# All clamps of the first FFN's weights on GpSimd as (min, max), and the casts of the first block's g and of the first two blocks' x on ScalarE

## The chip, the core and the metric

The kernel runs on one core of one Trainium2 chip. The metric is the device time of one execution in microseconds, lower is better. The engines are TensorE (PE; PEld is its weight load), VectorE (DVE), ScalarE (ACT), GpSimd (POOL) and SyncE (SP), which issues the DMAs. Each engine has one queue of instructions, taken in order; engines wait for each other by semaphores.

## The reference

Attention with a causal window of 64 tokens (4 sequences of 576 tokens, 8 heads of 64), a first feed-forward layer with ELU, an RMS norm, and a second, gated feed-forward layer. The part that the change touches is the first layer:

```python
def _moe_ref(x, w_in, w_out):          # x [2304, 512], w_in [512, 2048], w_out [2048, 512]
    h = x @ w_in
    g = np.where(h > 0.0, h, np.exp(np.minimum(h, 0.0)) - 1.0)
    return g @ w_out
```

The inputs and the result are wider than what one matmul takes: the weights arrive in 8-byte words of which the kernel reads both 32-bit halves, and the matmuls run on pairs (a rounded part and the remainder).

## The kernel before, in words

Every matmul operand of the feed-forward layers is split in two: a rounded part (a cast to the matmul's type) and what is left (a subtraction). A product is then three matmuls: rounded by rounded, remainder by rounded, rounded by remainder.

*The feeder of weights* (class `Feeder`, object `fw1` for the first layer, with `pool=True`; `fwp` for the second, with `pool=False`). A unit is a 128 x 512 piece of `w_in` or `w_out`; the first layer has 32 of them. Each passes through three stages, one `step()` apart:

- `s1`: ACT makes the magnitude from the high half (L311, into a tile `wm`, of which there are three) and scales the low half in place (L312); then a clamp to `MAX_M` (L314), by DVE for even units and by POOL for odd ones where `pool` is set, always by DVE for the second layer; then DVE shifts and joins the halves (L316).
- `s2`: DVE sets the sign (L323), and `nc.any` casts the rounded part (L331), on ACT or DVE, whichever the planner picks.
- `s3`: the remainder is subtracted, by POOL in the first layer (L337).

A unit's raw tile is loaded by SP up to four units ahead (L304) and comes free after `s2`.

*The first layer* runs over 6 blocks of 384 tokens. In each block 16 steps f: `mm_in` (12 matmuls, L381) gives h in PSUM; `elu` makes g with two ACT steps (L399, L400) and one of DVE (L401), and `split_g` casts it (L390, through its argument `copy`, here always DVE) and subtracts (L391, DVE); two steps later (`LAG`) `mm_y` multiplies g by `w_out` (12 matmuls, L408). Only in block 0 are the units of `fw1` made: two `step()`s in each f. The split weights then stay for the other blocks. Beside each of the first five blocks runs the attention for the next one, in slots between the steps (`att_*`, L164 to L239), which fills the next x; `x_split` casts the 4 parts of x (L364, DVE) and subtracts (L365, DVE), for block 0 ahead of the loop and for each later block at the end of the block before.

*Blocks 1 to 4* also hold the preparation of the second layer's weights (`prep_matrix`, `prep_out`: `fwp.s1`, the sign, and combinations by POOL, written to DRAM). Then the second layer follows.

*Order.* The program's order is not the order on the engines: a planner lays the instructions out on the queues by a modelled timeline and also picks the engine of each `nc.any` operation. Once laid out, each queue is fixed.

Of the kernel before, what the change touches and what calls it, by code (L numbers as in the profile page):

```python
# [13 lines left out]
ALU = mybir.AluOpType  # L14
# [6 lines left out]
def kernel(  # L21
# [17 lines left out]
    nc = tc.nc  # L39
# [10 lines left out]
    BLOCKS1 = [384]*6  # L50
    MAX_M = (2.0 - 2.0 ** -20) * 2.0 ** 15 / 2.0 ** 112
# [26 lines left out]
    def psum(tag, bufs):  # L78
        if starting[0] and tag == "w":
            tag, bufs = (("w", 4), ("y", 4))[starting[1] % 2]  # L80
            starting[1] += 1
        return ps.tile([128, 512], F32, tag=tag, name=tag, bufs=bufs)
# [162 lines left out]
    def att_schedule(u0, n, xt, nslots, gap):  # L245

        tail = 4 + 2 * gap
        slots = {}

        def put(s, key, f):  # L250
            slots.setdefault(s, []).append((key, f))

        first = 2
        pitch = max(1.0, (nslots - 1 - tail - first) / max(1, n - 1))
        for i in range(n):
            u = u0 + i
            sb = first + int(i * pitch)
            put(sb - 2, 0, lambda u=u: att_a(u))
            put(sb, 1, lambda u=u: att_b(u))
            for h in range(2):  # L260
                e = sb + h * gap
                put(e, 0.5, lambda u=u, h=h: att_e(u, h))
                put(e + gap - 1, 3, lambda u=u, h=h: att_n(u, h))
                put(e + gap, 4, lambda u=u, h=h: att_c(u, h))
            put(sb + 2 * gap + 2, 5, lambda u=u, o=i * 128: att_d(u, xt, o))
        return {s: [f for _, f in sorted(v, key=lambda z: -z[0])] for s, v in slots.items()}
# [17 lines left out]
    class Feeder:  # L284
# [23 lines left out]
        def s1(self, i):  # L308
            lo, hi = self.r[i][:, :, 0], self.r[i][:, :, 1]
            m = mp.tile([128, 512], F32, tag="wm", name="wm", bufs=3)  # L310
            nc.scalar.activation(out=m, in_=hi.bitcast(F32), func=AF.Abs, scale=2.0 ** -112)  # L311
            nc.scalar.activation(out=lo, in_=lo.bitcast(U32), func=AF.Copy, scale=0.875 * 2.0 ** -29,  # L312
                bias=0.4999)
            (nc.gpsimd if self.pool and i % 2 else nc.vector).tensor_scalar(  # L314
                out=m, in0=m, scalar1=MAX_M, scalar2=None, op0=ALU.min)
            nc.vector.scalar_tensor_tensor(  # L316
                out=m.bitcast(I32), in0=m.bitcast(I32), scalar=3, in1=lo,
                op0=ALU.logical_shift_left, op1=ALU.bitwise_or)
            self.m[i] = m
# [37 lines left out]
                self.step()  # L357


    def x_split(xt, n):  # L360
        r = []
        for kk in range(KD):
            xk = mp.tile([128, 2, NMAX], F32R, tag=f"x{kk}", name=f"x{kk}")
            nc.vector.tensor_copy(out=xk[:, 0, :n], in_=xt[:, kk, :n])  # L364
            nc.vector.tensor_tensor(  # L365
                out=xk[:, 1, :n], in0=xt[:, kk, :n], in1=xk[:, 0, :n].bitcast(F32),
                op=ALU.subtract)
            r.append(xk)
        return r

    def mm_in(pt, wt, xs, n, by_k=False):

        seq = []
        for kk in range(KD):
            seq += [(kk, 0, 0), (kk, 1, 0)]
        for kk in range(KD):
            seq += [(kk, 0, 1)]
        if by_k:
            seq.sort(key=lambda z: z[0])
        for i, (kk, a, c) in enumerate(seq):  # L380
            nc.tensor.matmul(  # L381
                pt[:, :n], lhsT=wt[:, a, kk * 128:(kk + 1) * 128], rhs=xs[kk][:, c, :n],
                start=(i == 0), stop=(i == len(seq) - 1))

    def x_tile():
        return mp.tile([128, KD, NMAX], F32, tag="xt", name="xt")

    def split_g(src, n, copy):
        g = mp.tile([128, 2, NMAX], F32R, tag="g", name="g", bufs=1 + LAG)
        copy(out=g[:, 0, :n], in_=src[:, :n])  # L390
        nc.vector.tensor_tensor(  # L391
            out=g[:, 1, :n], in0=src[:, :n], in1=g[:, 0, :n].bitcast(F32), op=ALU.subtract)
        return g


    def elu(ph, n):

        e = mp.tile([128, NMAX], F32, tag="e", name="e", bufs=2)
        nc.scalar.activation(out=e[:, :n], in_=ph[:, :n], func=AF.Relu, scale=-1.0)  # L399
        nc.scalar.activation(out=e[:, :n], in_=e[:, :n], func=AF.Exp, scale=-1.0)  # L400
        nc.vector.scalar_tensor_tensor(  # L401
            out=e[:, :n], in0=e[:, :n], scalar=-1.0, in1=ph[:, :n], op0=ALU.add, op1=ALU.max)
        return split_g(e, n, nc.vector.tensor_copy)

    def mm_y(py, wt, g, n, first, last):
        for i, (a, c) in enumerate(((0, 0), (1, 0), (0, 1))):
            for m in range(KD):
                nc.tensor.matmul(  # L408
                    py[m][:, :n], lhsT=wt[:, a, m * 128:(m + 1) * 128], rhs=g[:, c, :n],
                    start=(first and i == 0), stop=(last and i == 2))  # L410
# [65 lines left out]
    def x_load(sb):  # L476
        t0 = 2 * NB * sb
        xa = mp.tile([128, 2, 2 * NB], F32, tag="xt", name="xa")
        xb = f2p.tile([128, 2, 2 * NB], F32, tag="xb", name="xb")
        for h, t in enumerate((xa, xb)):  # L480
            nc.sync.dma_start(out=t, in_=xspill[:, 2 * h:2 * h + 2, t0:t0 + 2 * NB])
        xab[0], xab[1] = xa, xb
# [126 lines left out]
    def p_load(n):  # L609
        i, j = n // 7, ORDER[n % 7]  # L610
        u = wp.tile([128, 2, 2, 256], F32R, tag="wu", name="pu")
        nc.sync.dma_start(
            out=u.rearrange("p a b c -> p (a b c)").bitcast(F32), in_=pspill[:, n, :])
        U[i, j] = u
# [139 lines left out]
    xt = x_tile()  # L754
# [7 lines left out]
        load_v(t)  # L762
    for s in range(NSTART):
        fw1.step()
    xs = x_split(xt, BLOCKS1[0])

    tok0 = 0
    pend = []
    nblk = len(BLOCKS1)
    for b, n in enumerate(BLOCKS1):  # L770
        last = b == nblk - 1
        slots = {}
        if not last:
            nn = BLOCKS1[b + 1]
            xt = x_tile()
            slots = att_schedule((tok0 + n) // 128, nn // 128, xt, 2 * F1 - 1, 3)
        else:
            att_stack.close()
            f2p = ctx.enter_context(tc.tile_pool(name="f2p", bufs=1))
            x_load(0)  # L780
            for j in range(AHEAD2):
                slots.setdefault(14 + 2 * j, []).append(lambda n=j: p_load(n))
            for j in range(len(prep_o) // 2):
                slots.setdefault(PS0 + (31 - PS0) * j // (2 * F2), []).append(prep_o.pop(0))
            xi = x_items()
            for j, fn in enumerate(xi[:5]):
                slots.setdefault(15 + 3 * j, []).append(fn)
            x_late += xi[5:]
        if b and not last:
            for i in range(PREP_PER):  # L790
                if prep:
                    slots.setdefault(PS0 + (31 - PS0) * i // PREP_PER, []).append(prep.pop(0))
        for i, f in enumerate(pend):
            slots.setdefault(NS0 + NSP * i, []).insert(0, f)
        py = [psum("y", 4) for _ in range(KD)]
        gs = {}

        def run_slot(s):
            for f in slots.get(s, []):
                f()  # L800

        for f in range(F1):
            fw1.until(("in", f))
            ph = psum("w", 4)
            mm_in(ph, wu[("in", f)], xs, n, f == F1 - 1)
            gs[f] = elu(ph, n)
            run_slot(2 * f)
            if f == F1 - 1 and not last:
                xs_next = x_split(xt, nn)
            if b == 0:  # L810
                fw1.step()
            if f >= LAG:
                fw1.until(("out", f - LAG))
                mm_y(py, wu[("out", f - LAG)], gs.pop(f - LAG), n, f == LAG, False)
            run_slot(2 * f + 1)
            if b == 0:
                fw1.step()
        for f in range(F1 - LAG, F1):
            fw1.until(("out", f))
            mm_y(py, wu[("out", f)], gs.pop(f), n, False, f == F1 - 1)  # L820
        if last:
            for fn in x_late:
                fn()
        pend = norm_items(py, n, tok0, last)
        if not last:
            xs = xs_next
        tok0 += n
# [87 lines left out]
```

## Time and profile before

| | |
|---|---|
| median of 3 runs | 968.45 us (966.33 to 969.38) |
| the profiled execution, its time | 967.15 us |
| its span, first to last instruction | 965.4 us |
| PE busy | 918.5 us (95%) |
| DVE busy | 650.4 us (67%) |
| ACT busy | 491.9 us (51%) |
| POOL busy | 211.8 us (22%) |

The profile is of one execution. An engine's busy time is the time in which it has an instruction at work; a wait is idle time of an engine put down to what ended last before it went on. Shares over the whole span mix stages: block 0 of the first layer, which alone makes weights, lies at about 40 to 143 us, the other blocks of the first layer up to about 540, the second layer from there to the end. A duration of DVE or POOL also holds time in which the instruction had begun and stood still.

### The profile page before, as it was taken

Reading aid. Unit: us, or ns where it says so; the run is one execution under the profiler, and the core shown is the slowest. Engines: PE = TensorE matmul, PEld = TensorE weight load, DVE = VectorE, ACT = ScalarE, POOL = GpSimd, SP = SyncE. Lnnn points to the kernel's source line nnn. Section 1 sums busy time; section 2 is a strip of 40 time slices with the busy share of each in tenths; the row PEclk is TensorE's granted clock in tenths of the full one; section 3 lists DMA queues with packets and bytes.
Section 4 is the critical chain, followed back from the end, with each engine's and each line's share of the span. In section 5 each row is a group of like instructions: output and inputs, shape, how many; then the busy total and the mean of one; then the engine's idle time right before and its main releaser. Section 6 shows DMA issues by size and latency. Waiting matters only on the chain.

```text
span 965.4 us, 16449 instructions
## 1 busy us (share of the span) xinstructions
PE 918.5 (95%) x5916; PEld 863.7 (89%) x5916; DVE 650.4 (67%) x1451; ACT 491.9 (51%) x1199; POOL 211.8 (22%) x228
## 2 busy tenths in 40 slices
PE   6678889999999999999999999999999999999998
PEld 5577789988889998899999999899998998998996
DVE  3899997858867786787788488178363276561461
ACT  5887755665666656566545456344141442341440
POOL 2465760146236114404402100200000000000000
PEclk9789989999999999999999999999999999999999
DMA  9556531765474265536438719781984737945621
GB/s 234 165 167 199 133 108 23 221 194 159 146 228 145 78 197 172 156 103 199 159 122 286 262 48 385 283 349 48 404 328 143 278 124 243 371 141 208 240 70 66
DMA packets 150402, 183.02 MB, mean 190 GB/s; under 512 B 81712, under 2 KB 111408, under 8 KB 150320
## 3 DMA queue, kind: packets, MB, share of 16 engines
q1 hardware_dynamic: 150320, 181.96, 57.3%
q8 instruction: 47, 0.77, 0.3%
q14 instruction: 35, 0.29, 0.1%
HBM read 144.18 MB, written 37.75 MB: 188 GB/s over the span
## 4 chain that ended last, share of the span: by engine, by line
PE 67%; DMA 6%; POOL 4%; ACT 4%; DVE 4%; issue 1%; SPq 0%; POOLq 0%; DVEq 0%; ACTq 0%
PE y L669 16%; PE w L669 12%; PE y L408 11%; PE w L381 10%; PE y L703 10%; PE w L703 5%; DMA pspill<-stg 5%; POOL stg L540 2%; ACT s L206 1%; ACT stg L539 1%; PE w L164 1%; POOL sw L569 1%; PE w L235 1%; PE w L222 1%; PE w L187 1%
## 5 line engine op out<-in xcount | busy, mean ns | idle before, releaser
L381 PE MATMUL w<-x,wu 128*128 128x384 f32 x1152 | 226.8, 345 | 15.3 <-DVE e L401 5.7
L408 PE MATMUL y<-g,wu 128*128 128x384 f32 x1152 | 223.7, 340 | 5.6 <-DVE g L390 3.0
L381 PEld LDWEIGHTS w<-x,wu 128*128 128x128 f32 x1152 | 203.8, 192 | 21.4 <-DVE e L401 6.1
L408 PEld LDWEIGHTS y<-g,wu 128*128 128x128 f32 x1152 | 198.6, 188 | 10.1 <-DVE g L390 4.2
L669 PE MATMUL y<-xw,pu 128*128 128x384 f32 x864 | 161.6, 334 | 0.0
L669 PEld LDWEIGHTS y<-xw,pu 128*128 128x128 f32 x864 | 151.2, 188 | 0.8
L540 POOL TENSOR_TENSOR stg<-wm,stg 128x256 fp32r<-128x256 f32 x72 | 62.5, 873 | 299.9 <-ACT stg L539 299.9
L669 PE MATMUL w<-xw,pu 128*128 128x384 f32 x648 | 123.7, 334 | 0.0
L635 DVE TENSOR_TENSOR c<-c,w 128x384 f32<-128x384 f32 x72 | 39.6, 550 | 118.1 <-PE w L669 117.3
L669 PEld LDWEIGHTS w<-xw,pu 128*128 128x128 f32 x648 | 113.3, 188 | 0.3
L703 PE MATMUL y<-wu,g 128*128 128x512 f32 x432 | 106.4, 390 | 0.0
L703 PEld LDWEIGHTS y<-wu,g 128*128 128x128 f32 x432 | 80.9, 188 | 16.2
L401 DVE SCALAR_TENSOR_TENSOR e<-e,w 128x384 f32<-128x384 f32 x96 | 52.6, 549 | 51.3 <-ACT e L400 50.1
L631 ACT COPY c<-y 128x384 f32<-128x384 f32 x72 | 34.5, 482 | 67.9 <-PE y L669 67.3
L391 DVE TENSOR_TENSOR g<-e,g 128x384 fp32r<-128x384 f32 x96 | 66.0, 689 | 1.8
L399 ACT ACTIVATE e<-w 128x384 f32<-128x384 f32 x96 | 46.3, 484 | 37.2 <-PE w L381 37.1
L337 POOL TENSOR_TENSOR wu<-wm,wu 128x512 fp32r<-128x512 f32 x32 | 47.3, 1489 | 42.7 <-ACT wu L331 27.6
L703 PE MATMUL w<-wu,g 128*128 128x512 f32 x216 | 55.9, 390 | 0.0
L651 ACT CAST g<-e 128x384 fp32r<-128x384 f32 x69 | 34.7, 511 | 37.5 <-DVE e L645 37.5
L206 ACT ACTIVATE s<-s,st 128x128 f32<-128x128 f32 x120 | 46.7, 392 | 10.9 <-DVE st L202 10.9
L640 ACT ACTIVATE e<-c 128x384 f32<-128x384 f32 x54 | 27.5, 524 | 47.1 <-DVE c L635 47.1
L400 ACT ACTIVATE e<-e 128x384 f32<-128x384 f32 x96 | 50.4, 526 | 1.7
(127 smaller groups left out, 1209.1 us busy)
## 6 DMA issues: line engine op xcount, KB each, us to landing
pu<-pspill SPq DMA_DIRECT2D x126, 512.0 KB, 6.5
pspill<-stg SPq DMA_DIRECT2D x84, 256.0 KB, 2.1
wu<-ospill SPq DMA_DIRECT2D x36, 512.0 KB, 5.2
big<-in_moe_w_out_dram SPq DMA_DIRECT2D x16, 512.0 KB, 5.3
big<-in_moe_w_in_dram SPq DMA_DIRECT2D x15, 512.0 KB, 3.8
vw<-in_v_dram SPq DMA_DIRECT2D x27, 256.0 KB, 3.6
tmp<-in_moe_w_out_dram SPq DMA_DIRECT2D x12, 512.0 KB, 4.7
big<-in_moe_w_gate_dram SPq DMA_DIRECT2D x12, 512.0 KB, 5.4
```

What stands on the lines that cost most here:

```text
L206: nc.scalar.activation(out=s[:, p, :], in_=s[:, p, :], func=AF.Exp, scale=-1.0, bias=st[:, 0, p, :], accum_out=st[:, 1, p, :])
L337: eng.tensor_tensor(out=u[:, 1, :], in0=m, in1=u[:, 0, :].bitcast(F32), op=ALU.subtract)
L381: nc.tensor.matmul(pt[:, :n], lhsT=wt[:, a, kk * 128:(kk + 1) * 128], rhs=xs[kk][:, c, :n], start=(i == 0), stop=(i == len(seq) - 1))
L391: nc.vector.tensor_tensor(out=g[:, 1, :n], in0=src[:, :n], in1=g[:, 0, :n].bitcast(F32), op=ALU.subtract)
L399: nc.scalar.activation(out=e[:, :n], in_=ph[:, :n], func=AF.Relu, scale=-1.0)
L400: nc.scalar.activation(out=e[:, :n], in_=e[:, :n], func=AF.Exp, scale=-1.0)
L401: nc.vector.scalar_tensor_tensor(out=e[:, :n], in0=e[:, :n], scalar=-1.0, in1=ph[:, :n], op0=ALU.add, op1=ALU.max)
L408: nc.tensor.matmul(py[m][:, :n], lhsT=wt[:, a, m * 128:(m + 1) * 128], rhs=g[:, c, :n], start=(first and i == 0), stop=(last and i == 2))
L540: nc.gpsimd.tensor_tensor(out=t[:, 1, :], in0=src, in1=t[:, 0, :].bitcast(F32), op=ALU.subtract)
L635: nc.vector.tensor_tensor(out=t, in0=t, in1=bank[b, qi][:, :NB], op=ALU.add)
L669: nc.tensor.matmul(bank[key][:, :NB], lhsT=u[:, qi, a, kk * 128:(kk + 1) * 128], rhs=X[j][kk][:, x, :], start=(first and n == 0), stop=(n ...
L703: nc.tensor.matmul(po[m], lhsT=g[:, a, (m % 3) * 128:(m % 3 + 1) * 128], rhs=w[:, x, :], start=(first and i == 0), stop=(last and i == 2))
```

## The change

All 32 clamps of the first layer's weights are given to POOL, in place of the 16 of odd units. The clamp itself becomes an instruction with two operations, min with `MAX_M` and then max with 0; its input is an absolute value, so the second one changes no number. The second layer's clamps stay on DVE and take the two operations as well. In block 0 the cast of g goes to ACT (16 instructions); the cast of x goes to ACT for block 0 (ahead of the loop) and for block 1 (at the end of block 0), 4 instructions each. The other blocks keep DVE for both. The subtractions stay where they are.

```diff
-            (nc.gpsimd if self.pool and i % 2 else nc.vector).tensor_scalar(
-                out=m, in0=m, scalar1=MAX_M, scalar2=None, op0=ALU.min)
+            (nc.gpsimd if self.pool else nc.vector).tensor_scalar(
+                out=m, in0=m, scalar1=MAX_M, scalar2=0.0, op0=ALU.min, op1=ALU.max)
...
-    def x_split(xt, n):
+    def x_split(xt, n, copy=nc.vector.tensor_copy):
...
-            nc.vector.tensor_copy(out=xk[:, 0, :n], in_=xt[:, kk, :n])
+            copy(out=xk[:, 0, :n], in_=xt[:, kk, :n])
...
-    def elu(ph, n):
+    def elu(ph, n, copy):
...
-        return split_g(e, n, nc.vector.tensor_copy)
+        return split_g(e, n, copy)
...
-    xs = x_split(xt, BLOCKS1[0])
+    xs = x_split(xt, BLOCKS1[0], nc.scalar.copy)
...
-            gs[f] = elu(ph, n)
+            gs[f] = elu(ph, n, nc.vector.tensor_copy if b else nc.scalar.copy)
...
-                xs_next = x_split(xt, nn)
+                xs_next = x_split(xt, nn, nc.vector.tensor_copy if b else nc.scalar.copy)
```

## Rows read from the trace of the kernel before

**Rows 1.** The page's part 1: busy us, share of the span, instructions.

```profile
PE 918.5 (95%) x5916; PEld 863.7 (89%) x5916; DVE 650.4 (67%) x1451; ACT 491.9 (51%) x1199; POOL 211.8 (22%) x228
```

**Rows 2.** Busy time by stretch: us, engines' busy us (instructions), granted clock, DMA share, GB/s.

```profile
40.00:143.00 103.00, 85.20 (x600) 78.79 (x600) 100.02 (x193) 74.02 (x173) 65.96 (x43) 0.92 0.52 154
143.00:540.00 397.00, 386.23 (x2851) 369.56 (x2852) 307.75 (x746) 235.94 (x621) 121.84 (x143) 1.00 0.53 165
```

**Rows 3.** Waits in 40 to 143 us: engine, tile, line <- releaser: us, times, longest.

```profile
POOL wu L337 <- ACT wu L331: 27.6, 15, 3.2
ACT wu L331 <- DVE wm L323: 16.1, 12, 3.2
...
PE w L381 <- DVE e L401: 5.7, 2, 4.5
...
PE w L381 <- DVE x L364: 3.3, 1, 3.3
...
ACT big L312 <- DMA big<-in_moe_w_out_dram: 3.0, 2, 1.5
ACT big L312 <- DMA big<-in_moe_w_in_dram: 2.8, 3, 1.3
ACT tmp L312 <- DMA tmp<-in_moe_w_out_dram: 2.7, 3, 2.0
...
ACT wm L311 <- DMA big<-in_moe_w_out_dram: 1.0, 1, 1.0
```

**Rows 4.** The chain that ended last, at 143 us: start, us, what.

```profile
143.33 2.43 PE y L408 x12
```

**Rows 5.** Groups of DVE in 40 to 143 us: busy us, mean ns, idle before.

```profile
L390 DVE CAST g<-e 128x384 fp32r<-128x384 f32 x15 | 11.7, 779 | 0.4
...
L314 DVE TENSOR_SCALAR wm<-wm 128x512 f32<-128x512 f32 x13 | 9.0, 690 | 0.0
...
L364 DVE CAST x<-xt 128x384 fp32r<-128x384 f32 x4 | 3.3, 892 | 0.0
```

**Rows 6.** Lines 390 and 314, whole span: ns min/median/max, first and last start.

```profile
L390 DVE CAST g<-e x96: 344/360/1454, 57.3 to 548.5; 128x384 fp32r<-128x384 f32 x96
...
L314 DVE TENSOR_SCALAR wm<-wm x52: 395/426/1514, 15.9 to 605.7; 128x512 f32<-128x512 f32 x52
L314 POOL TENSOR_SCALAR wm<-wm x16: 1490/1768/2044, 20.3 to 136.7; 128x512 f32<-128x512 f32 x16
```

**Rows 7.** POOL's timeline, its first subtractions: start, us, [idle before <- releaser].

```profile
34.20 3.86 POOL L337 TENSOR_TENSOR wu<-wm,wu 128x512 fp32r<-128x512 f32 x3 [12.15 <-DVE wu L331]
```

**Rows 8.** Line 651, second layer, ACT's cast of 384 columns: columns as in rows 6.

```profile
L651 ACT CAST g<-e x69: 494/514/526, 570.3 to 940.4; 128x384 fp32r<-128x384 f32 x69
```

**Rows 9.** Other POOL lines, 337 and 90: columns as in rows 6.

```profile
L337 POOL TENSOR_TENSOR wu<-wm,wu x32: 1267/1448/1860, 34.2 to 143.0; 128x512 fp32r<-128x512 f32 x32
...
L90 POOL TENSOR_SCALAR_AFFINE_SELECT mask<-mask x6: 287/290/293, 1.3 to 4.5; 64x128 f32<-64x128 f32 x6
```

**Rows 10.** Stretches: all engines as in rows 2; then L337's POOL; then L314's DVE, POOL.

```profile
34.20:144.40 110.20, 91.25 (x698) 84.14 (x696) 103.63 (x197) 80.64 (x184) 73.08 (x47) 0.91 0.48 144
...
34.20:144.40 110.20, 47.34 (x32) 0.91 0.48 144
...
34.20:144.40 110.20, 9.40 (x14) 26.20 (x15) 0.91 0.48 144
...
143.00:540.00 397.00, 13.11 (x31) 0.00 (x0) 1.00 0.53 165
```

**Rows 11.** Timelines of DVE and POOL around 108 and 121 us: columns as in rows 7.

```profile
107.72 1.59 POOL L314 TENSOR_SCALAR wm<-wm 128x512 f32<-128x512 f32 x1
108.77 0.82 DVE L314 TENSOR_SCALAR wm<-wm 128x512 f32<-128x512 f32 x1
...
118.96 3.47 POOL L337 TENSOR_TENSOR wu<-wm,wu 128x512 fp32r<-128x512 f32 x2 [1.23 <-DVE st L214]
...
121.22 1.49 DVE L314 TENSOR_SCALAR wm<-wm 128x512 f32<-128x512 f32 x1
```

## The prediction, made before the changed kernel ran

> **What bounds the kernel now.** I read the page's busy shares first [rows 1]: TensorE (PE) is busy for 95% of the 965.4 us span, so the change can only be worth what PE loses somewhere. The table of stretches [rows 2] says where. From 143 to 540 us PE is busy 386.2 of 397 us; from 40 to 143 us only 85.2 of 103, at a granted clock of 0.92 against 1.00 later. That stretch is the first block of the first FFN, in which the weights are being split as they arrive. There the fullest engine is VectorE (DVE): 100.0 of 103 us. ScalarE (ACT) has 74.0, GpSimd (POOL) 66.0. The waits of that stretch agree [rows 3]: the longest of PE's are for DVE's e and DVE's x, the longest of ACT's is 16.1 us for DVE's signed weight, and POOL's 27.6 us are for the ACT cast that stands behind that same DVE step. So DVE is the bound of block 0, ACT and POOL wait in its wake, and the chain of waits shows it handing over to PE at 143.3 us [rows 4]. After that PE hardly waits: what block 0 gains goes to the end of the kernel one for one.
>
> **The change, part by part.**
>
> *Taken off DVE.* In the stretch 40 to 143 us stand 13 clamps (9.0 us), 15 of the 16 casts of g (11.7 us) and the 4 casts of the first block's x (3.3 us) [rows 5]: 24.0 of DVE's 100.0 us. They cost more here than they do alone: the cast of g has a median of 360 ns over the kernel but a mean of 779 here [rows 5, 6]. The difference is time in which a DVE instruction waits for POOL, and it leaves with the instruction. The other three clamps and the casts of the second block's x lie at the edges, and I cost them at nothing. The early clamps become 1.49 - 0.43 = 1.06 us longer on a POOL that sits idle for 12.15 us ahead of its first subtraction at 34.2 us [rows 7], and the x that the first weights meet isn't cast before 40 us (all four casts stand in that stretch [rows 5]); were a weight wanted at once, the price would be that 1.06 us. The casts at the end of the block are 4 x (514 - 360) ns = 0.6 us longer on ACT, beside the last matmuls of the block; without that cover they cost the 0.6 us.
>
> *Put on ACT.* The 19 casts of that stretch, at 514 ns each (the same cast of 384 columns by ACT in the second FFN [rows 8]), are 9.8 us: 74.0 + 9.8 = 83.8 us.
>
> *Put on POOL.* 16 more clamps of 512 columns, 14 of them in this stage. The clamp that POOL now does takes 1.49 us at least and 1.77 in the middle [rows 6], more than the subtraction of two tensors of the same size, 1.27 us at least [rows 9], so it isn't held by the data it reads. The new form has two operations, and no row shows that on POOL. Low bound: the select over 128 columns takes 0.29 us [rows 9], so 512 columns are 1.16 us even if none of it is a fixed cost. High bound: the second operation costs all that the first does, 2.98. The nearest row is the single clamp, undisturbed: I take 1.49 and keep both ends. POOL's work runs from the first subtraction at 34.2 us to the last at 144.4; its 32 subtractions take 47.3 us [rows 10]. With 29 clamps in that time (14 by DVE and 15 by POOL now [rows 10]) it has 47.3 + 29 x 1.49 = 90.5 of 110.2 us.
>
> *Contention.* A clamp on POOL also delays DVE. Two pairs of rows show how much: the DVE clamp at 121.22 us, begun under a POOL subtraction, takes 1.49 us, 1.06 over its median of 0.43; the one at 108.77 us, begun under a POOL clamp, takes 0.82, only 0.39 over [rows 6, 11]. 14 more chances of up to 0.39 us are at most 5.5 us; only part of them meet an instruction that minds, and the waits that leave with the moved instructions are already in the 24.0. I take 2 us, with 0 to 5.5 as ends: DVE about 78 of 103.
>
> The Trainium skill (SBUF — State Buffer, section Who interferes with whom) speaks against the change: GpSimd and a DVE instruction that copies, casts or reads two SBUF tensors exclude each other for the whole instruction. The rows agree on the subtraction and not on the clamp, where the wait is 0.39 of 1.59 us. By the rows 2 us are lost; by that rule the shared-access rival below would come true.
>
> *Elsewhere.* The clamps of the second FFN's weights stay on DVE and get a second operation: some 36 instructions, 31 of them in 143 to 540 us [rows 10]. Lower bound nothing, upper a doubling, 0.43 us each, 15 us in all, spread where DVE is busy 307.7 of 397 us [rows 2]. The work of PE hides it, so I take nothing; if nothing hid it, 15 us.
>
> *The sum.* What is late next? DVE falls to 78, PE's own work is at most 85.2 and less at full clock. ACT has 83.8 and still waits for weights to arrive: 3.0 + 2.8 + 2.7 + 1.0 = 9.5 us in that stretch [rows 3], which this change doesn't touch. 83.8 + 9.5 = 93.3, so ACT sets the pace and the 103 us become 93.3: a gain of 9.7 us. POOL would set a longer pace only if packed tighter than I allow: at 95% of the 110.2 - 9.7 = 100.5 us it may have 95.5, that is (95.5 - 47.3) / 29 = 1.66 us a clamp. Against the profiled execution, 967.15 us (span 965.4), this gives 957.5; the median of the runs lies 1.3 above it, so **958.8, said as 958.5**. If the waits for weights vanish too and the planner hands a few free copies to DVE (casts of weights, which may go to either engine), ACT at 97% like DVE today needs 83.8 / 0.97 = 86.4: gain 16.6, 952. If about half of the gain is lost to ACT waiting in line for DVE's e ahead of each cast of g, with the feeder's two ACT steps queued behind it, the gain is 4 to 5: 964. The case spans 951 to 964.5.
>
> **The rivals.**
>
> *POOL becomes the pace.* If the clamp costs what it does in the middle, 26.2 / 15 = 1.75 us [rows 10], POOL has 47.3 + 50.8 = 98.1 of 110.2 us; in order, waiting for ACT's copies in between, it packs to 95% at best, 103.3, a gain of 6.9, and to 100% of today's time at worst, a gain of nothing. 961.5 to 971, middle 965.5. For: POOL's idle time today is all waiting. Against: those waits are for DVE's wake.
>
> *The shared access decides (slower).* If POOL and DVE really exclude each other while either runs, the sum that counts is theirs together. DVE loses 14 clamps and 19 casts at their own 0.43 and 0.36 us, 12.9; POOL gains 14 x 1.49 = 20.9. The stage is 8 us longer, 976.5; it decides from a clamp of 12.9 / 14 = 0.92 us upward. For: the 1.06 us under the subtraction. Against: the 0.39 under the clamp, and 103.6 + 73.1 us of work by the two in 110.2 us today [rows 10, 11]. 971 to 981.
>
> *The two operations cost double (slower).* At 2.98 us POOL has 47.3 + 86.4 = 133.7 us; at 95% 140.7, against 110.2: 30 us later, 999. It decides above (110.2 x 0.95 - 47.3) / 29 = 1.98 us a clamp. For: the single operation is already slower than the data asks. Against: the select and the subtraction aren't. 983 to 1003.
>
> *Nothing moves.* ACT stands in line behind DVE as often as DVE is relieved, or the planner, seeing ACT full, gives its free copies to DVE: the load only changes its name. 965.5 to 971.
>
> **How the numbers follow.** Forecast 0.60; POOL the pace 0.14; shared access 0.08; double price 0.10; nothing moves 0.08. About 0.3% (2.9 us) is what a measurement can tell from no change, so faster means under 965.5, slower over 971.4. Faster: 0.60 + half of 0.14 = 0.67, and 0.02 of the fourth, 0.69. Same: the other half, 0.07, and 0.06: 0.13. Slower: 0.08 + 0.10 = 0.18. The range 950 to 972 holds the forecast, POOL's case and the one of no effect; the two slower ones are left out.
>
> **What would show it.** Right: DVE no longer over 95% busy in the first block; ACT the fullest; PE's waits for e and x gone; PE continuous from about 133 us instead of 143; POOL's clamp under 1.66 us; the time from there to the end unchanged at about 822 us. Wrong: a clamp of about 2 us or more and PE waiting for POOL's weights (double price); DVE's remaining two-tensor steps longer on average than today (shared access); DVE falling by 24 us and PE starting its continuous run at 143 all the same (ACT's line); or second-FFN clamps on DVE well over 0.43 us with PE waiting after 143.

## The result, and the profile of the changed kernel

The changed kernel takes 975.71 us (median; 974.88 to 977.18) beside 968.4 us for the kernel before: a ratio of 1.0079, 95% interval 1.0065 to 1.0092. It is slower by 7.3 us; the forecast was a gain of 9.7. By its number it falls to the shared-access rival (976.5); by what the profile shows it is closest to "nothing moves" (965.5 to 971), 4.7 us beyond that case's end.

The page's busy shares of the changed kernel (columns as in [rows 1]; profiled execution 974.88 us, span 973.1):

```profile
PE 921.2 (95%) x5916; PEld 862.1 (89%) x5916; DVE 637.5 (66%) x1410; ACT 502.7 (52%) x1224; POOL 207.4 (21%) x244
```

Its table of stretches (columns as in [rows 2]):

```profile
40.00:143.00 103.00, 81.62 (x577) 72.55 (x575) 83.54 (x150) 77.45 (x182) 56.03 (x51) 0.95 0.53 153
143.00:540.00 397.00, 383.69 (x2829) 365.43 (x2827) 305.86 (x738) 237.66 (x624) 124.03 (x145) 1.00 0.51 158
```

Beside [rows 2], block 0 has DVE at 83.5 instead of 100.0 of 103 us and POOL at 56.0 instead of 66.0, ACT at 77.5 instead of 74.0. No engine is as full as DVE was, and PE got fewer matmuls done in the same 103 us: 577 against 600. POOL's last subtraction begins at 152.9 us against 143.0 [rows 9]. Cutting the stretch at 80 us shows that two opposite things happened. First the kernel before, then the changed one (same columns):

```profile
40.00:80.00 40.00, 32.02 (x240) 29.85 (x240) 38.82 (x74) 29.67 (x69) 24.25 (x16) 0.87 0.54 169
80.00:143.00 63.00, 53.18 (x360) 48.94 (x360) 61.20 (x119) 44.35 (x105) 41.72 (x28) 0.95 0.50 144
```

```profile
40.00:80.00 40.00, 35.32 (x273) 32.14 (x271) 36.09 (x77) 34.03 (x88) 19.66 (x19) 1.00 0.59 169
80.00:143.00 63.00, 46.30 (x306) 40.41 (x304) 47.45 (x74) 43.41 (x96) 36.37 (x32) 0.92 0.49 142
```

Up to 80 us the change does what was forecast: 33 matmuls more, at a granted clock of 1.00 instead of 0.87. After 80 us it gives back 54, with DVE at 47 of 63 us and ACT at 43 of 63: everybody waits for somebody. By 160 us it is 27 matmuls behind the kernel before (936 against 963 since the start). The waits of 40 to 143 us say for whom (columns as in [rows 3]):

```profile
POOL wm L314 <- ACT wm L311: 25.7, 14, 4.2
POOL wu L337 <- ACT wu L331: 20.1, 16, 4.5
...
ACT wu L331 <- DVE wm L323: 8.5, 7, 1.8
PE w L381 <- ACT wu L331: 8.3, 4, 3.4
...
DVE e L401 <- ACT e L400: 7.6, 6, 2.2
...
ACT big L312 <- DMA big<-in_moe_w_in_dram: 5.0, 6, 1.7
...
PE y L408 <- ACT wu L331: 4.8, 2, 2.6
...
DVE g L391 <- ACT g L390: 4.2, 3, 2.6
PE y L408 <- ACT g L390: 4.0, 4, 1.5
...
PE w L381 <- DVE e L401: 1.4, 1, 1.4
...
ACT g L390 <- DVE e L401: 0.8, 1, 0.8
```

PE's wait for DVE's x of [rows 3] is gone and that for DVE's e is down to 1.4 us; PE now waits for ACT's weight cast (L331) and ACT's cast of g. ACT's wait for DVE's sign has halved from 16.1 us [rows 3]. DVE, which hardly stood idle before, now waits for ACT. And POOL's clamp, which every unit now has, waits 25.7 us for ACT's magnitude (L311), against 6.5 in the same stretch of the kernel before:

```profile
POOL wm L314 <- ACT wm L311: 6.5, 3, 3.4
```

### The profile page after: what moved, and what is told of

It reads as the page before. It is cut to its first block, busy times and chain, and to the rows that moved or that the text cites. A ratio compares the mean times of both kernels' runs of the same rounds, so it can differ in the third digit from the quotient of the medians.

```text
span 973.1 us, 16447 instructions
## 1 busy us (share of the span) xinstructions
PE 921.2 (95%) x5916; PEld 862.1 (89%) x5916; DVE 637.5 (66%) x1410; ACT 502.7 (52%) x1224; POOL 207.4 (21%) x244
## 4 chain that ended last, share of the span: by engine, by line
PE 68%; DMA 9%; ACT 6%; DVE 6%; POOL 4%; issue 2%; SPq 0%; POOLq 0%; ACTq 0%; DVEq 0%
PE y L669 15%; PE w L669 12%; PE y L408 11%; PE w L381 11%; PE y L703 10%; PE w L703 5%; DMA pspill<-stg 5%; POOL stg L540 2%; ACT s L206 2%; DVE wm L323 1%; PE w L235 1%; PE w L164 1%; DVE x L365 1%; DMA big<-in_moe_w_out_dram 1%; DMA big<-in_moe_w_in_dram 1%
## 5 line engine op out<-in xcount | busy, mean ns | idle before, releaser
L408 PE MATMUL y<-g,wu 128*128 128x384 f32 x1152 | 226.4, 342 | 10.6 <-ACT wu L331 4.8
L381 PEld LDWEIGHTS w<-x,wu 128*128 128x128 f32 x1152 | 199.1, 188 | 28.2 <-ACT wu L331 11.8
L703 PEld LDWEIGHTS y<-wu,g 128*128 128x128 f32 x432 | 80.9, 188 | 16.1
L401 DVE SCALAR_TENSOR_TENSOR e<-e,w 128x384 f32<-128x384 f32 x96 | 52.8, 550 | 54.7 <-ACT e L400 53.5
L391 DVE TENSOR_TENSOR g<-e,g 128x384 fp32r<-128x384 f32 x96 | 69.8, 727 | 7.6 <-ACT g L390 5.8
L337 POOL TENSOR_TENSOR wu<-wm,wu 128x512 fp32r<-128x512 f32 x32 | 46.4, 1455 | 36.6 <-ACT wu L331 21.8
```

What stands on the lines that cost most here:

```text
L337: eng.tensor_tensor(out=u[:, 1, :], in0=m, in1=u[:, 0, :].bitcast(F32), op=ALU.subtract)
L381: nc.tensor.matmul(pt[:, :n], lhsT=wt[:, a, kk * 128:(kk + 1) * 128], rhs=xs[kk][:, c, :n], start=(i == 0), stop=(i == len(seq) - 1))
L391: nc.vector.tensor_tensor(out=g[:, 1, :n], in0=src[:, :n], in1=g[:, 0, :n].bitcast(F32), op=ALU.subtract)
L401: nc.vector.scalar_tensor_tensor(out=e[:, :n], in0=e[:, :n], scalar=-1.0, in1=ph[:, :n], op0=ALU.add, op1=ALU.max)
L408: nc.tensor.matmul(py[m][:, :n], lhsT=wt[:, a, m * 128:(m + 1) * 128], rhs=g[:, c, :n], start=(first and i == 0), stop=(last and i == 2))
L703: nc.tensor.matmul(po[m], lhsT=g[:, a, (m % 3) * 128:(m % 3 + 1) * 128], rhs=w[:, x, :], start=(first and i == 0), stop=(last and i == 2))
```

## The experiments

Each ratio is against the kernel before, measured beside the run, with its 95% interval; the kernel before has a median of 967.5 to 969.2 us in these measurements. A difference of two runs in us is one of their medians.

### The parts alone

e1 has the clamps of the change without its casts:

```diff
-    xs = x_split(xt, BLOCKS1[0], nc.scalar.copy)
+    xs = x_split(xt, BLOCKS1[0])
-            gs[f] = elu(ph, n, nc.vector.tensor_copy if b else nc.scalar.copy)
+            gs[f] = elu(ph, n, nc.vector.tensor_copy)
-                xs_next = x_split(xt, nn, nc.vector.tensor_copy if b else nc.scalar.copy)
+                xs_next = x_split(xt, nn)
```

> All clamps of the first layer on GpSimd as (min, max), every cast as before on VectorE. Theory A (ScalarE's line: the moved casts stand in ScalarE's queue and hold up the weights behind them): without the casts the clamp's 0.6 us is pure relief, so 962 to 966 us, and TensorE's 15 us of waits for ScalarE's weight casts fall under 5. Theory B (the clamp's extra trip to GpSimd lengthens each unit's path): the whole loss is here, 974 to 978. Theory C (each edit makes the planner lay the queues out anew, and that scatter is what is measured): anything between 960 and 978, and the three parts do not add up to the whole.

Measured: 971.37 us, 1.0040 [1.0023, 1.0058].

e2 has the casts of the change, and the clamps as before:

```diff
-            (nc.gpsimd if self.pool else nc.vector).tensor_scalar(
-                out=m, in0=m, scalar1=MAX_M, scalar2=0.0, op0=ALU.min, op1=ALU.max)
+            (nc.gpsimd if self.pool and i % 2 else nc.vector).tensor_scalar(
+                out=m, in0=m, scalar1=MAX_M, scalar2=None, op0=ALU.min)
```

> The casts of block 0's g and of the first two blocks' x on ScalarE, clamps as before (odd units on GpSimd with one operation, 1.5 to 1.8 us). Theory A: the whole loss is here, 974 to 980 us. Theory B: as VectorE loses 12 to 15 us of casts in a stage that it bounds, 960 to 966. Theory C: anything between.

Measured: 969.66 us, 1.0022 [1.0007, 1.0037].

e3 changes nothing but the clamp's form; odd units stay with POOL:

```diff
-                out=m, in0=m, scalar1=MAX_M, scalar2=None, op0=ALU.min)
+                out=m, in0=m, scalar1=MAX_M, scalar2=0.0, op0=ALU.min, op1=ALU.max)
```

> Only the form of the clamp: odd units stay on GpSimd and even ones on VectorE, both as (min, max). GpSimd's clamp falls from 1.75 us to 0.6 to 0.8. Theory A: a small gain, 964 to 968 us, as GpSimd was not the bound. Theory B: the same, 964 to 968, since no unit takes a new trip. Theory C: the layout changes although the work hardly does, so up to 8 us either way.

Measured: 966.47 us, 0.9988 [0.9973, 1.0003].

e4 is e1 with the clamp in its old form of one operation:

```diff
-                out=m, in0=m, scalar1=MAX_M, scalar2=0.0, op0=ALU.min, op1=ALU.max)
+                out=m, in0=m, scalar1=MAX_M, scalar2=None, op0=ALU.min)
```

> All clamps on GpSimd with one operation (1.5 to 1.8 us), casts on VectorE. Against e1 this gives the price of the form: 29 clamps x 1.0 us = 29 us more of GpSimd's time. Theory A: GpSimd at 47 + 51 = 98 of 110 us becomes the pace, e1 + 3 to 8 us. Theory B: the longer trip counts in full for each unit, e1 + 8 us or more. Theory C: no fixed sign against e1.

Measured: 970.75 us, 1.0030 [1.0016, 1.0044].

e12 is the changed kernel with the casts of g back on DVE (the diff is the middle one of e1's three edits):

> The changed kernel with block 0's casts of g back on VectorE: all clamps on GpSimd and only the 8 casts of x on ScalarE. If the casts of g are what puts ScalarE's queue on the path, 966 to 970 us, under e1's 971.4; if the clamp's trip through GpSimd is, 970 to 973, like e1.

Measured: 977.08 us, 1.0088 [1.0067, 1.0110].

What follows. Line 314 over the whole span of the changed kernel and of e4 (columns as in [rows 6]):

```profile
L314 POOL TENSOR_SCALAR wm<-wm x32: 606/669/1052, 16.2 to 146.6; 128x512 f32<-128x512 f32 x32
```

```profile
L314 POOL TENSOR_SCALAR wm<-wm x32: 1479/1704/2056, 16.5 to 143.5; 128x512 f32<-128x512 f32 x32
```

With its second operation POOL's clamp takes 0.61 us at least and 0.67 in the middle: less than half of the one-operation form, and less than the low bound of the prediction. So the double price is out. And the price does not matter: in 40 to 143 us e1 and e4 have POOL busy for 59.8 and 83.4 us,

```profile
40.00:143.00 103.00, 86.20 (x586) 78.36 (x585) 91.45 (x170) 73.44 (x169) 59.80 (x52) 0.92 0.51 154
```

```profile
40.00:143.00 103.00, 86.01 (x589) 76.30 (x589) 97.19 (x178) 72.45 (x168) 83.35 (x54) 0.95 0.53 154
```

and end 0.6 us apart, within each other's interval. POOL's fullness is not what holds this block. Theories A and B, each with a fixed cause, give ranges that hold neither e1 nor e2, and e12 misses both of its ranges too; only theory C, the planner's layout, allows all of e1 to e4. Each part costs a little alone, and their sum, 0.40% and 0.22%, is near the whole's 0.79%. But the steps between them have sizes that no work accounts for: with the clamps there, 8 casts of x cost 0.48% (e1 to e12), and 16 casts of g then nothing (e12 to the whole, -0.09%). That points to the layout, for which see the controls below.

### What DVE's steps lose to POOL

The prediction let a moved instruction take its wait along. The DVE groups of 40 to 143 us (columns as in [rows 5]) say otherwise. The kernel before, then the changed one:

```profile
L323 DVE SCALAR_TENSOR_TENSOR wm<-big,wm 128x512 int32<-128x512 int32 x18 | 14.6, 817 | 0.1
...
L391 DVE TENSOR_TENSOR g<-e,g 128x384 fp32r<-128x384 f32 x14 | 10.8, 774 | 0.1
...
L323 DVE SCALAR_TENSOR_TENSOR wm<-tmp,wm 128x512 int32<-128x512 int32 x11 | 8.4, 765 | 0.1
```

```profile
L323 DVE SCALAR_TENSOR_TENSOR wm<-big,wm 128x512 int32<-128x512 int32 x14 | 14.9, 1063 | 0.3
L391 DVE TENSOR_TENSOR g<-e,g 128x384 fp32r<-128x384 f32 x14 | 13.7, 984 | 4.2 <-ACT g L390 4.2
L323 DVE SCALAR_TENSOR_TENSOR wm<-tmp,wm 128x512 int32<-128x512 int32 x11 | 12.9, 1168 | 0.1
```

The sign (L323) and the subtraction of g (L391) have not changed, and a sign takes 0.25 to 0.40 us longer, a subtraction 0.21. They now stand beside a POOL subtraction, as the moved casts and clamps did. To count it, one sums over all DVE instructions that begin from 34 to 160 us what each takes above the shortest of its own line and shape in that kernel, and then counts only those that begin while a POOL subtraction is at work:

```
DVE time above each form's own minimum, 34 to 160 us
before 32.0   after 30.6   e1 31.1   e2 30.0   e3 30.8   e4 34.5   e12 32.6
of it in instructions begun under a POOL subtraction
before 23.9   after 24.2   e1 22.4   e2 24.3   e3 24.8   e4 24.1   e12 24.0
```

Neither sum follows the number of DVE instructions (193 in 40 to 143 us before, 150 after). The second one is 22 to 25 us in all seven kernels, 0.7 to 0.8 us for each of POOL's 32 subtractions; most of the rest stands in instructions begun under POOL steps with one input (6.6 us before, 5.1 after). (The expectations of e9 and e16 speak of 27 to 32 and of 28 us; counted as here, the first sum is 30 to 35.) Two runs take the subtractions away. e9 puts into the kernel before, in place of POOL's subtraction, an instruction with one input (the remainder of the first layer's weights is left out with it):

```diff
-            eng.tensor_tensor(
-                out=u[:, 1, :], in0=m, in1=u[:, 0, :].bitcast(F32), op=ALU.subtract)
+            eng.tensor_scalar(
+                out=u[:, 1, :], in0=u[:, 0, :].bitcast(F32), scalar1=MAX_M, scalar2=0.0,
+                op0=ALU.min, op1=ALU.max)
```

> The kernel before with GpSimd's subtraction of two tensors replaced by a clamp of the rounded part (one input, min and max); this leaves out the remainder of the first layer's weights, whose place in the matmuls stays. VectorE's time above its own durations in the stage is 27 to 32 us in every kernel so far, whichever instructions were moved: if it belongs to the 32 subtractions it falls under 10 us here. If VectorE's busy time sets block 0 of the kernel before, the stage is then some 15 us or more shorter, 948 to 956 us; if the queues' mutual waiting sets it, 962 to 969 although VectorE is 20 us emptier.

Measured: 956.29 us, 0.9886 [0.9864, 0.9908], 12.9 us less, 0.3 us above the first range. DVE's time above the minimum falls from 32.0 to 14.1 us, not under 10 as expected: 11.7 us of it stand in instructions begun under POOL's one-input instructions, of which this kernel has 48. PE does 713 matmuls from 40 to 143 us, at a granted clock of 1.00:

```profile
40.00:143.00 103.00, 94.66 (x713) 85.99 (x710) 92.97 (x221) 79.39 (x185) 44.33 (x42) 1.00 0.55 159
```

So in the kernel before DVE is the bound, as the prediction said, and the thing to take off it is the wait, not the clamps and casts. (e9 also takes POOL's time from 1.45 to 0.64 us an instruction. That this isn't the cause is argued from e1 beside e4 and from e3, where POOL's clamps are about 1 us longer or shorter and the time changes by 0.1%.)

e10 makes the same edit in the changed kernel:

> The same edit in the changed kernel, leaving out the same. If waits for shared access are what made the changed kernel slower, it gains more than the kernel before does, 945 to 957 us. If the loss is in the order and the mutual waiting of ScalarE, VectorE and GpSimd, it stays above e9 by 5 us or more.

Measured: 979.13 us, 1.0114 [1.0091, 1.0137]. DVE's time above the minimum is 8.4 us; DVE is busy for 64 of 103 us,

```profile
40.00:143.00 103.00, 80.22 (x566) 72.14 (x564) 64.48 (x149) 78.76 (x184) 42.47 (x51) 0.93 0.50 152
```

and the kernel is 3.4 us slower, not faster. The changed kernel still has the contention, but to take it away brings nothing: something else sets the pace.

### What sets the pace after the change

The chain of waits of e10, here 8.7 us of it (start, us, what):

```profile
86.71 3.81 DMA big<-in_moe_w_in_dram
...
90.54 0.65 ACT big L312
91.19 0.41 ACT e L401
91.61 0.47 ACT pT L224
92.08 0.52 ACT wu L331
92.59 0.42 ACT g L391
...
93.04 0.04 DVE g L392
...
93.62 0.69 DVE wm L316
...
94.33 1.00 DVE wm L323
95.33 0.02 SPq L304
...
95.40 3.70 DMA big<-in_moe_w_in_dram
```

It is a closed loop (e10 has one line more, so its L391, L392, L401 are lines 390, 391 and 400). The sign of a unit frees its raw tile, one of three named "big"; SP at once issues the load of a later unit into it, 3.7 to 3.8 us; ACT scales it (L312); behind that stand, in ACT's one queue, an exp, a copy of the attention, a weight cast and now the cast of g; DVE's subtraction of g waits for that cast; the shift (L316) and the sign stand behind it in DVE's queue; the sign frees a tile. The changed kernel's chain goes through a similar turn, with a magnitude (L311) in place of the exp and the weight cast:

```profile
86.16 1.10 DVE wm L323
87.26 0.02 SPq L304
...
87.32 3.76 DMA big<-in_moe_w_in_dram
...
91.09 0.67 ACT big L312
91.76 0.47 ACT pT L224
92.23 0.56 ACT wm L311
92.79 0.41 ACT g L390
...
93.22 0.04 DVE g L391
...
93.82 1.83 DVE wm L316
...
95.67 0.70 DVE wm L323
```

After that sign it leaves the loop: ACT's weight cast at 96.39 us, PE's matmuls at 97.07.

The loop isn't new: in the kernel before, too, SP waits for the sign ahead of its loads, 79.1 us in 40 to 143 against 68.6 after. What is new is that the cast of g lies in it as a step of another engine, with a wait in that engine's line. By the program's order the even units' clamps do so too, but POOL is in neither of the stretches shown. A mean over the third to the nineteenth tile "big", from the issue of its load to the end of its sign, is 19.0 us in the kernel before and 20.6 in the changed one (e1 20.1, e2 19.2, e3 18.8, e10 20.2, e12 21.1, e9 16.5).

Two things keep this from being a proof. With three such tiles always in use, a longer block makes a longer life of each, whatever holds the block up. And from 40 to 158 us the chain passes through a load of raw weights eight times in e10, four times in the changed kernel and once in the kernel before, but also five times in e17 below, the fastest kernel of all. So the loop is shown at work in e10; that it costs the changed kernel its time is argued.

e5 gives the loop room in the changed kernel, with the first 25 units' raw tiles taken from another pool:

```diff
-    fw1 = Feeder(w1src, lambda: big4() if fw1.loaded % 2 or fw1.loaded > 24 else tmp4(), lambda i: unit(), AHEAD, pool=True)
+    fw1 = Feeder(w1src, lambda: big4() if fw1.loaded > 24 else tmp4(), lambda i: unit(), AHEAD, pool=True)
```

with `tmp4` handing out tiles of the pool `wp`.

> The changed kernel, with the raw tiles of the first 25 units taken from the big pool of weight slots, so that no load waits for one of three raw tiles. In before and after alike every such load is issued 0.06 us after the sign step of the unit three tiles earlier. Ring theory (the stage runs at three raw tiles per lifetime of a raw tile, 18.9 us before and 20.6 after): the loads run ahead, ScalarE's waits for DMA (10 us) vanish, the block-0 stage ends at about 140 us or earlier instead of 153, 960 to 967 us. Line theory (ScalarE's queue in order holds the weights up, whatever the loads do): 973 to 979 as the changed kernel itself.

Measured: 970.08 us, 1.0010 [0.9997, 1.0023]: 5.6 us less than the changed kernel, but in neither theory's range. SP's wait for signs falls from 68.6 to 26.9 us (SP then waits 46.3 us for PE, ahead of loads of the attention); ACT's waits for DMA, from 40 to 160 us, fall from 11.7 to 5.8.

e7 does the same to the kernel before:

> The kernel before with the raw tiles freed as in e5. Ring theory, in its strong form (the ring set the pace before too, and VectorE's 97% was a coincidence): 955 to 963 us. In its weak form (VectorE set the pace before, the ring only after the change): 965 to 970, no change. Line theory: no change, 965 to 970.

Measured: 974.66 us, 1.0056 [1.0040, 1.0072]. DVE is busy there for 101.4 of 103 us; the ring wasn't its bound. But no theory allowed for a slower kernel: the edit that takes 5.6 us off the changed kernel adds 6.2 to the one before (968.51 beside it). So e5's gain is no larger than what this edit does without a known reason.

e6 and e8 also give `wm`, the working tile, more buffers for the first 20 units, after and before:

```diff
-            m = mp.tile([128, 512], F32, tag="wm", name="wm", bufs=3)
+            if self.pool and i < 20:
+                m = wp.tile([128, 1024], F32, tag="wu", name="wm")[:, :512]
+            else:
+                m = mp.tile([128, 512], F32, tag="wm", name="wm", bufs=3)
```

> The same, and the magnitude tiles wm of the first 20 units also from the pool of weight slots, so that neither ring (three raw tiles, three wm) holds a unit back. Ring theory: what e5 leaves for the wm ring comes off, VectorE is again the fullest engine, 952 to 962 us. Line theory: 973 to 979.

> The kernel before with both rings freed as in e6. Ring theory, strong form: 950 to 962 us. Weak form: 964 to 970, as VectorE is at 97% already. Line theory: 965 to 970. If e6 falls under this one, the change's relief of VectorE is real and was only hidden by the rings; if e6 stays above it by 5 us or more, the loss has another cause.

Measured: 1006.73 us (1.0397) and 996.69 us (1.0288). Both are far slower; DVE is busy for only 52.9 of 103 us in e6. The extra tiles come from the pool of 32 slots that also holds the split weights, so one limit may have been put in place of another; whether that or the planner's layout is to blame was not tried. These two say nothing of the ring.

The other candidate is ACT's load. e13 takes the feeder's weight casts off ACT in the changed kernel, e14 the same in e10:

```diff
-            nc.any.tensor_copy(out=u[:, 0, :], in_=m)
+            (nc.vector if self.pool else nc.any).tensor_copy(out=u[:, 0, :], in_=m)
```

> The changed kernel with the first layer's weight casts put on VectorE for good (27 of 32 of them are on ScalarE in it, 16.6 us). Theory ScalarE's queue is the pace: ScalarE falls to about 61 us of the stage, VectorE rises by 11 to 95, a unit needs no trip to ScalarE between sign and subtraction, 962 to 969 us. Theory layout: 970 to 982, no fixed sign. Theory trip of the clamp: the clamp's trip stays, 973 to 978.

> The same on top of e10 (which leaves out the remainder of the first layer's weights and took 979 us with VectorE busy for only 64 of 103 us). If ScalarE's queue is the pace there, it falls by 15 us or more, to 950 to 962. If a layout is to blame, anything from 960 to 985.

Measured: 971.80 us (1.0049 [1.0031, 1.0067]) and 978.40 us (1.0112 [1.0090, 1.0133]). e13 is 3.9 us under the changed kernel, above the range that ACT's queue as the pace would give, and no more than the swap below does. In e14 ACT has 64.8 and DVE 76.7 of 103 us, both far from full, and the time is that of e10. So it isn't how much ACT has to do.

### How much of it is the layout

Every edit gives the planner another problem, and it may lay out the queues otherwise. As a control e11 (on the changed kernel) and e15 (on the kernel before) write two independent ACT steps of a unit in the other order. The program asks for the same steps; the planner gave three copies or fewer to another engine for it:

```diff
-            nc.scalar.activation(out=m, in_=hi.bitcast(F32), func=AF.Abs, scale=2.0 ** -112)
             nc.scalar.activation(out=lo, in_=lo.bitcast(U32), func=AF.Copy, scale=0.875 * 2.0 ** -29,
                 bias=0.4999)
+            nc.scalar.activation(out=m, in_=hi.bitcast(F32), func=AF.Abs, scale=2.0 ** -112)
```

> A control: the changed kernel with the two ScalarE steps of a unit written in the other order (the low half first). The work of every engine is the same, and the planner lays the queues out anew. If the loss of the changed kernel is an accident of its layout, this one is anywhere from 962 to 982; if it follows from where the work lies, 973 to 979.

> A control: the kernel before with a unit's two ScalarE steps written in the other order. The same work, laid out anew. The same edit moved the changed kernel by 3.9 us. If the layout's scatter is of that size here too, 964 to 973 us.

Measured: 971.79 us (1.0046 [1.0022, 1.0070]) and 972.00 us (1.0044 [1.0028, 1.0060]). The swap takes 3.9 us off the changed kernel and adds 4.0 to the one before. Written in the other order, the change costs nothing (971.79 against 972.00) instead of 7.3 us.

### The change with POOL's subtraction gone

If DVE's waits belong to POOL's two-tensor subtraction, giving that to DVE should cost 32 instructions of about 0.68 us and return the waits. e16 does it to e1, e17 to the changed kernel, and e18 is e16 with the swap of e11:

```diff
-            eng = nc.gpsimd if self.pool else nc.vector
-            eng.tensor_tensor(
+            nc.vector.tensor_tensor(
                 out=u[:, 1, :], in0=m, in1=u[:, 0, :].bitcast(F32), op=ALU.subtract)
```

> All clamps on GpSimd as (min, max), and the subtraction of each unit on VectorE in place of GpSimd, casts as before. If VectorE's waits belong to GpSimd's subtractions, they fall from 28 us to under 8 us, which pays for the 32 x 0.69 = 22 us that VectorE takes over; with the clamps gone (6 us) VectorE's stage is about as full as before, but the last trip of a unit is gone: 958 to 967 us. If the waits go with GpSimd's clamps as well, 972 to 985.

> The changed kernel with the units' subtractions on VectorE: e16 plus the casts of block 0's g and of the first two blocks' x on ScalarE. If VectorE's busy time is again what sets the pace (94 of 103 us in e16), the casts take 8 us off it and this is 953 to 959 us. If the casts cost by putting ScalarE between two VectorE steps (12.6 us of its waits and TensorE's for g), it is 962 to 972, above e16's 960.8.

> A control: e16 with a unit's two ScalarE steps written in the other order. The same edit moved the kernel before by +4.0 us and the changed one by -3.9. If e16's gain is of its work, 957 to 965 us; if it was a lucky layout, 965 to 972.

Measured: e16 960.82 us (0.9932 [0.9911, 0.9953]), e17 955.27 us (0.9856 [0.9842, 0.9871]), e18 964.41 us (0.9944 [0.9922, 0.9966]). e17 is faster than both kernels: 13.8 us under the one before, 20.4 under the changed one. Block 0 of e17:

```profile
40.00:143.00 103.00, 95.04 (x708) 87.64 (x709) 93.48 (x222) 89.91 (x218) 23.81 (x26) 1.00 0.53 155
```

```profile
L336 DVE TENSOR_TENSOR wu<-wm,wu 128x512 fp32r<-128x512 f32 x28 | 19.8, 707 | 3.0 <-ACT wu L331 2.9
...
L323 DVE SCALAR_TENSOR_TENSOR wm<-big,wm 128x512 int32<-128x512 int32 x17 | 13.3, 782 | 0.0
...
L316 DVE SCALAR_TENSOR_TENSOR wm<-wm,big 128x512 int32<-128x512 int32 x17 | 11.6, 681 | 0.0
```

DVE does the subtraction in 0.71 us where POOL needed 1.45 [rows 9]; its sign is back at 0.78 us; its time above the minimum is 8.8 us (e16 and e18 10.2, where under 8 was expected). 19.8 us of subtractions came to it and some 22 us of waits left it, and PE got 708 matmuls done instead of 600. Here the casts on ACT seem to pay: e17 differs from e16 by them alone and is 5.5 us under it by the medians, 0.76% by the ratios. That is more than the swap moved a kernel anywhere (0.44% at most; e18 lies 3.6 us over e16, 0.12% by the ratios) and than e7 was moved without a known reason (0.56%), though not by much, and e17 itself was measured in one order only.

One comparison keeps the waits from being the whole story. e10 and e17 have the same clamps and casts, and in both DVE's time above the minimum is down to 8.4 and 8.8 us, yet they lie 23.9 us apart. In e17 a unit has one trip less, as POOL's subtraction is gone from its path; in e10 that step is still there. How much of the 23.9 us is this trip and how much the layout was not tried.

## Why the prediction was wrong, point by point

*What bounds the kernel: right.* DVE held block 0 (at the very end ACT steps stand between it and PE: the chain goes from DVE's sign at 140.59 us over ACT's weight cast at 142.29 and its step on e at 142.91 to PE at 143.33), and what block 0 gains reaches the end: e9 and e17 do 113 and 108 matmuls more from 40 to 143 us and end 12.9 and 13.8 us sooner.

*Taken off DVE: the step that failed.* Of the 24.0 us of [rows 5] only 13 x 0.43 + 19 x 0.36 = 12.4 us were the instructions' own; the other 11.6 were waits for POOL, and "it leaves with the instruction" was an assumption that no row bore. The waits went to other DVE steps, above all to the sign and the subtraction of g: DVE steps begun under a POOL subtraction lose 23.9 us before and 24.2 after. DVE's busy time fell by 16.5 us, and part even of that is work not reached: 25 signs in the stretch against 29. The row that would have warned stood in the profile: the cast of g at 779 ns against a median of 360 [rows 5, 6] says that any DVE step in that place waits, not that this one does.

*The sum: the second step that failed.* It asked which engine is fullest next and let ACT run at 83.8 us of work plus 9.5 of waits for DMA. ACT is at 77.5, for it got through fewer units, and its waits for DMA are 11.7 us; its casts of g took the 0.51 us forecast. What came next was no engine's sum: the fullest engine has 83.5 of 103 us, and PE waits for ACT's weight cast (8.3 + 4.8 us) and ACT's cast of g (4.0). In e10 and e14 every engine has over a fifth of the stretch to spare, and the kernel takes 979.1 and 978.4 us; the chain of e10 is a loop of waits through four queues. That the same loop holds the changed kernel is argued. The sentence on "waiting in line for DVE's e ahead of each cast of g" comes nearest, with half of the gain as its price, but it has the wait the wrong way round: ACT's cast of g waits 0.8 us for DVE's e, while DVE waits 7.6 us for ACT's exp and 4.2 for its cast of g. The lead of 33 matmuls at 80 us and the loss of 54 after it show that waits take all of the gain.

*POOL's price: too high and beside the point.* 0.61 to 0.67 us, not 1.49; e4 pays 1.70 and is as fast as e1. The low bound of 1.16 us was no low bound: it is four times a select of 128 columns, and whatever part of that select is a fixed cost makes 512 columns cheaper than that.

*Contention: the right mechanism, put in the wrong account.* The Trainium skill (SBUF — State Buffer, section Who interferes with whom) has a DVE instruction with two SBUF inputs contend with a GpSimd instruction that reads SBUF, for a shared pair of ports that it calls an exclusive lock. For POOL's subtraction the runs agree: 22 to 25 us of DVE's time in block 0 stand in steps begun under one of the 32, held for up to 1.14 us. For a POOL clamp they don't: in the kernel before no DVE step begun under one is held for more than 0.44 us of the 1.5 to 2.0 that it takes. The row that the prediction read for this could not show it, as only 0.54 us of that clamp was left when the DVE step began. These do: two signs, each with two tensors, begin and end inside one clamp.

```profile
136.71 2.03 POOL L314 TENSOR_SCALAR wm<-wm 128x512 f32<-128x512 f32 x1 [2.14 <-ACT wm L311]
136.72 1.69 DVE L323 SCALAR_TENSOR_TENSOR wm<-big,wm 128x512 int32<-128x512 int32 x2
```

So the shared-access rival holds the measured time, but not for its reason: it was to decide from a clamp of 0.92 us upward, and with clamps of 0.61 us the kernel is slower and with 1.70 (e4 beside e1) no worse.

*Nothing moves: the nearest.* Its sign, DVE falling while PE starts its continuous run no sooner, is what the profile shows. Its mechanism isn't: ACT's wait for DVE's sign fell from 16.1 to 8.5 us, and the planner gave ACT 27 of the 32 weight casts, against 26 before, so no load went back to DVE. It stopped at 971 since no row suggested that an emptier DVE could go with a longer block.

*Elsewhere: right.* The second layer's clamps on DVE kept their 0.43 us with the second operation (36 of them, in the middle 426 ns).

*What stays open.* The two pairs of the change differ by 7.5 us, +7.3 and -0.2, for a swap that leaves the steps as they are. Shown is that neither has the gain, that DVE's waits for POOL's subtraction stay whatever is moved off it, and that in e10, with room on every engine, the chain goes round a loop. That the loop through the raw tiles costs the changed kernel the 7.3 us is argued from its chain, from the tiles' longer life and from e5's 5.6 us. e5's gain is not much larger than the swap's 3.9 and is smaller than the 6.2 that the same edit adds to the kernel before, so how much of the loss is the change's own and how much is an unlucky layout is not settled. Why the loop doesn't hold e17, whose casts lie in ACT's queue as well and whose chain passes through raw loads too, was not tried.

## What to carry to other kernels

Where an instruction takes longer in one stage than elsewhere, find what it waits for: here moving DVE's casts and clamps left the wait to the steps that stayed, and moving what they waited for (GpSimd's two-tensor subtraction) took most of it away. Before handing a step to an emptier engine, follow the buffer that it works on all the way round: in queues taken in order, each hand-over puts another engine's line into the loop that frees the buffer, and such a loop can be what is left with no engine full, as in e10. And where a planner lays out the queues, measure a second, equivalent order of the program: here it moved the time by 0.3 to 0.4% by itself, which is half of the whole effect.

## What the runs showed of the hardware that was not expected

A clamp of 128 x 512 on GpSimd takes 1.48 us at least with one operation (min) and 0.61 with two (min, max); e3, e4 and e1 show it with the same tiles, and so does the time from a clamp's start to that of POOL's next instruction: 1.45 us at least in e4, 0.58 in e1. On DVE both take 0.43 in the middle. GpSimd's subtraction of two such tensors costs DVE 0.7 to 0.8 us each, and the sum hardly depends on what DVE has to do meanwhile: 22 to 25 us over 32 subtractions in seven kernels, with 150 to 193 DVE instructions from 40 to 143 us. A GpSimd clamp of such a tensor costs a DVE step begun under it 0.44 us at most in the kernel before, although the clamp lasts 1.5 to 2.0 us.
